# Second-layer weights and tables ahead of the filter loads, eight tiles turned by DMA, a first tile copied by two engines, and a new planned order

## The chip, the core and the metric

The kernel runs on one core of one Trainium2 chip. The metric is device time in microseconds (us), the median over runs of the same program. The core has five engines that run side by side, each working through its own list of instructions strictly in order: PE (TensorE, matmuls), DVE (VectorE), ACT (ScalarE), POOL (GpSimd) and SP (SyncE, which here only issues transfers). Transfers between device memory and the on-chip buffer (SBUF) are carried by 16 DMA engines; SP, ACT and POOL can issue them. Matmuls write to PSUM, a small memory of eight banks, from which ACT or DVE copy the results out ("evacuate" them).

## What is computed

The output is the sum of three things: x itself, a spectral filter of the layer-normalised x (a two-dimensional real FFT, a product with complex weights W, the inverse FFT), and a two-layer perceptron of the same normalised x with a tanh GELU. x has 2048 rows and 640 columns, W 2048 x 321, the hidden layer 1536 columns; everything is bf16.

```python
def _A_ref(x, w_r, w_i):
    X = rfft2(x.astype(float32), axes=(-2, -1))
    X = X * (w_r + 1j * w_i)
    return irfft2(X, s=(S, D), axes=(-2, -1)).astype(bfloat16)

def _B_ref(x, w1, b1, w2, b2):
    h = gelu(einsum("bsd,df->bsf", x, w1) + b1)
    return einsum("bsf,fd->bsd", h, w2) + b2

x = A_x
xn = layernorm(x, axis=-1)
return x + _A_ref(xn, A_w_r, A_w_i) + _B_ref(xn, B_w1, B_b1, B_w2, B_b2)
```

## The kernel before

**Tiles.** x is held as 16 tiles of 128 rows (tile c has the rows 16p + c). The FFTs are matmuls with constant tables: G and H along the rows, E and GE along the columns, and the small M and N that join the sixteen tiles.

**Stage 1, tile by tile (DVE leads).** A tile is loaded (load_x). DVE takes its mean and variance (bn_stats, L567; bn_aggr, L569; ve = variance + 1e-5, L571). POOL raises ve to the power -1/2 (rstd, L572). DVE forms nmr = -mean x rstd (L574) and the normalised tile (L595). PE turns the tile over, five 128 x 128 transposes against an identity (L607), into one PSUM bank, and DVE or ACT copies it into xnT (L486 or L485, called from L612). The same normalised tile is folded on DVE (L618, L622) and multiplied by G on PE (L628), and the result goes into XV (L634). The buffers of normalised tiles hold two pairs of tiles (p_xn), so a pair takes the place of the pair two before it.

**Stage 2, the perceptron's first layer.** Blocks of 1, 1, 2, 2, 2, 4 and 4 tiles (BLOCKS) times 12 pieces of 128 hidden columns: five matmuls into one PSUM bank (L650), then a GELU on ACT into gT (L656). These sums have four banks to rotate through (ZONE "hps"). W1 arrives in three pieces (W1P).

**Stage 3, the spectral chain.** Its PE pieces have a fixed order (CHAIN): b pieces multiply XV by E and need XV of all sixteen tiles, c pieces apply M, DVE multiplies by the filter Wf (L723) and subtracts and adds (L727), d pieces apply N, copies bring the result into U, and SP turns U back into XV with DMA transposes (L748). Wf has 34 loads (load_w), 17 from A_w_r and 17 from A_w_i, and the first product waits for all of them.

**Stage 4, the second layer and the end.** Each output tile is a sum of 12 pieces gT x W2 (the function `second`), of H x the spectral result, of b2 and of x. For eight tiles (KEEP) gT x W2 is done ahead and added to b2bc by DVE (L824); for the other eight ACT copies b2bc (L803) into the place of the output. Either way POOL then adds x by an accumulating DMA (L826). b2bc is b2 spread to all 128 partitions by its load. DVE makes the last sum (L835), and SP stores (L838).

**The order.** The program is not written in the order in which it runs. Every operation is handed to a planner (Sched) with the engines that may do it, an estimated duration, a priority, and what it reads and writes. `schedule` runs through time with these estimates and, engine by engine, picks the operation that can start first, by priority among those within 0.03 us; it also decides, for a copy that DVE or ACT may do, which does it. For SP it keeps the order in which the operations were written down. A `gate` lets an operation be placed only after another one was placed; it is no wait on the chip, and neither is `late`, the earliest planned time. `sync` then puts semaphore waits where the data need them, and `emit` writes the five lists. On the chip an engine that reaches a wait stops, with all that is behind it in its list. All estimates bear on the order alone.

SP's list is thus: x tile 0, identity, tile 1, b1, W1's second piece, tiles 2 and 3, W1's third piece, G, the tiles 4 to 15 in pairs, E, M, N, the 34 filter loads, W2, GE, H, b2bc, then the transposes of U and the stores. ACT's list begins with the first piece of W1 (its DMA), then a table load for copies, and one for GELU ahead of the first GELU. POOL's has all nine rstd first, then the sixteen accumulating DMAs.

Of the kernel before, what the change touches and what calls it, by code (L numbers as in the profile page):

```python
# [13 lines left out]
D = 640  # L14
# [83 lines left out]
def act_us(n, ptr=0):  # L98
    return 0.055 + n / 1200.0 + 0.09 * ptr
# [57 lines left out]
class Sched:  # L157
# [36 lines left out]
    def schedule(self):  # L194
# [24 lines left out]
        while left:  # L219
            best = None  # L220
            for e in self.engines:
# [27 lines left out]
                if e == "sp":  # L249
                    t, o = min(cands, key=lambda c: c[1].seq)  # L250
                    if o is not min((p for p in pend[e] if not p.done), key=lambda p: p.seq):
                        continue
                else:
                    t0 = min(c[0] for c in cands)
                    near = [c for c in cands if c[0] <= t0 + 0.03]
                    if e == "pe" and self.mode != "128":
                        near = [c for c in cands if c[0] <= t0 + HOLD and c[1].alts and c[1].alts[0][0][0] == self.mode] or near
                    t, o = min(near, key=lambda c: (-c[1].prio, c[1].seq))
# [13 lines left out]
            if o.nbytes:  # L272
                if e == "pool":
                    o.end = t + 5.0
                else:
                    s = max(t + 0.9, dma_free)
                    dma_free = s + o.nbytes / o.rate
                    o.end = dma_free + 0.9
            else:
                o.end = t + dur + LAT[e]  # L280
# [96 lines left out]
W1P = [(0, 5), (5, 8), (8, 12)]  # L377
GROUPS = [(0, 2), (2, 3), (5, 3), (8, 3), (11, 3), (14, 2)]
BYDMA = ()
# [3 lines left out]
PRIO = {"hps": 10, "gelu": 50, "pb": 70, "pc": 80, "filt": 85, "ipc": 90, "eps": 60, "fin": 40}  # L383
# [4 lines left out]
HOME = (KEEP[:max(0, len(KEEP) - 7)] + tuple(c for c in range(15) if c not in KEEP))[:8]  # L388
WARM = (55, 12)


def bass_parallel_sum__spectral_gfnet__dense_activation_gelu__prompt_kernel(
# [21 lines left out]
    with ExitStack() as es:  # L414
# [27 lines left out]
        nmr = sb("nmr", [128, 16], F32)  # L442
# [25 lines left out]
        def load(dst, src, buf, nbytes, after=(), reads=(), rate=395e3, q="sp"):  # L468
            return K.op([(q, 0.45)], 400, lambda e, _: e.dma_start(dst, src), reads=reads, writes=[buf], after=after, nbytes=nbytes, rate=rate)  # L469
# [20 lines left out]
        K.op([("dve", 0.1)], 300, lambda e, _: e.memset(warm[:], 0.0), writes=[B_warm])  # L490
        K.op([("pool", 0.1)], 100, lambda e, _: e.memset(mhalf[:], -0.5), writes=[B_mh])
# [16 lines left out]
        def load_x(c, n, q="sp"):  # L508
            o = load(view(X, c * D, [[1, n * D]]), xv[:, c:c + n, :].rearrange("p c d -> p (c d)"), B_x[c], n * D * 256, q=q, rate=155e3 if c == 0 else 395e3)
            for i in range(1, n):  # L510
                B_x[c + i].writers.append(o)

        def load_w1(j, q="sp"):
            a, b = W1P[j]
            load(view(W1, 128 * a, [[F, 5], [1, 128 * (b - a)]]), w1v[:, :, 128 * a:128 * b], B_w1s[j], 163840 * (b - a), q=q, rate=300e3)
# [7 lines left out]
        load_w1(2)  # L523
        load(gtab[:], const["G"], B_g, 524288)
        for c in range(4, 16, 2):
            load_x(c, 2)
        load(etab[:], const["E"], B_e, 204800, rate=250e3)
        load(mtab[:], const["M"], B_m, 65536, rate=70e3)
        load(ntab[:], const["N"], B_n, 49152, rate=70e3)
        WP = 32 * KP  # L530

        def load_w(wsrc, p0, off, row, n, step):
            load(bass.AP(tensor=Wf, offset=p0 * WP + off, ap=[[2 * WP, 16], [2 * KP, n], [1, 321]]),
                 bass.AP(tensor=wsrc.tensor, offset=wsrc.offset + row * 321, ap=[[128 * 321, 16], [step * 321, n], [1, 321]]),
                 B_w, 16 * 642 * n, after=[wpad], rate=165e3)
# [12 lines left out]
        load(W2[:], w2v, B_w2, F * D * 2)  # L548
        load(getab[:], const["GE"], B_ge, 204800)
        load(htab[:].rearrange("p a b -> p (a b)"), const["H"], B_h, 524288)  # L550
        load(b2bc[:], bass.AP(tensor=b2v.tensor, offset=b2v.offset, ap=[[0, 128], [1, D]]), B_b2b, 163840)
# [3 lines left out]
        K.op([("dve", 0.08)], 200, lambda e, _: e.tensor_copy(b1col[:], psb(B_b1ps.slot, [[1, NFC]])), reads=[B_b1ps], writes=[B_b1c])  # L555
# [3 lines left out]
        norm_ops, ring_ops, a_ops = [], [], []  # L559
        B_rs = [Buf(f"rstd{c}") for c in range(16)]  # L560
        for c0, n in [(0, 1), (1, 1)] + [(c, 2) for c in range(2, 16, 2)]:
            pr = 100 - c0 / 2
            B_mv, B_ve, B_r = Buf("mv"), Buf("ve"), Buf("r")
            for c in range(c0, c0 + n):
                B_st = Buf("st")
                for h in range(2):
                    K.op([("dve", 0.393)], pr, lambda e, _, c=c, h=h: e.bn_stats(stats[:, c, 6 * h:6 * h + 6], view(X, c * D + H2 * h, [[1, H2]])),  # L567
                         reads=[B_x[c]], writes=[B_st])
# [4 lines left out]
                 reads=[B_ve, B_mh], writes=[B_r])  # L573
            K.op([("dve", 0.071)], pr, lambda e, _, a=a, b=b: e.scalar_tensor_tensor(out=nmr[:, a:b], in0=mv[:, a:b, 0], scalar=-1.0,  # L574
                                                                                     in1=rstd[:, a:b], op0=ALU.mult, op1=ALU.mult),
                 reads=[B_mv, B_r], writes=B_rs[a:b])
            for c in range(a, b):
                B_rs[c].writers += B_r.writers

        for pair in range(8):  # L580
# [10 lines left out]
            for n in range(2):  # L591
# [4 lines left out]
                    out=xnv(n, 0, [[1, D]]), in0=view(X, c * D, [[1, D]]), scalar1=rstd[:, c:c + 1], scalar2=nmr[:, c:c + 1], op0=ALU.mult, op1=ALU.add),  # L596
                    reads=[B_x[c], B_rs[c]], writes=[xn, B_xn])
                norm_ops.append(o)
                if c in BYDMA:
                    K.op([("sp", 1.6)], 0, lambda e, _, c=c, n=n, xnv=xnv: e.dma_start_transpose(xnT[:, :, 128 * c:128 * c + 128], xnv(n, 0, [[1, D]])),  # L600
                         reads=[B_xn, xn], writes=[B_xnT[c]], nbytes=163840, rate=150e3)
                    continue
                tps = Buf(f"tps{c}", psum, 1, ZONE["tps"])

                def xt(e, _, n=n, xnv=xnv, tps=tps):
                    for j in range(5):
                        ins = e.transpose(psb(tps.slot, [[1, 512]]).bitcast(BF)[:, 128 * j:128 * j + 128], xnv(n, 128 * j, [[1, 128]]), ident[:])  # L607
                    return ins
                tp = K.op([("pe", 5 * mm_us(128))], pr, xt, reads=[B_xn, xn, B_id], writes=[tps], alts=[[("128", 5 * mm_us(128))]])
                if not c:  # L610
                    idle(WARM[1], WARM[1] * mm_us(128), gate=[tp])
                K.op([("dve", 0.41), ("act", act_us(640))], pr,  # L612
                     copy(lambda c=c: xnT[:, :, 128 * c:128 * c + 128],
                          lambda tps=tps: psb(tps.slot, [[1, 512]]).bitcast(BF)[:, 0:640].rearrange("p (j t) -> p j t", j=5)),
                     reads=[tps], writes=[B_xnT[c]])
# [54 lines left out]
        def five_segs(n):  # L670
            return [("128", 4 * n * mm_us(Q4)), ("32", n * 0.075 + 0.01)]
# [5 lines left out]
        for gi, (c0, n) in enumerate(GROUPS):  # L677
# [8 lines left out]
            for v in range(2):  # L686
                K.op([("dve", dve_us(320 * n) + 0.05), ("act", act_us(320 * n) + 0.16)], PRIO["pb"] - c0 / 10,
# [184 lines left out]
```

## Time and profile before

| what | value |
|---|---|
| median of three runs | 157.81 us (157.73 to 157.98) |
| the profiled execution: span | 160.8 us |
| PE busy | 148.7 us (92% of the span) |
| DVE busy | 113.2 us (70%) |
| ACT busy | 84.0 us (52%) |
| POOL busy | 26.2 us (16%) |
| mean granted PE clock | 0.979 |

All views are of one profiled execution. It is 2.99 us longer than the median of the plain runs. In the profile a line such as `L474 PE MATMUL ps<-xnT,W 128*128 128x256 bf16 x40` reads: source line, engine, operation, what is written and read, shape, how many; PEld are the weight loads that go with the matmuls. Line 474 is the helper through which nearly all matmuls go, so they are told apart by their tiles: xnT,W is the first layer, W,gT the second, gtab,T the product with G, etab,XV the b pieces, Xb,mtab the c pieces, Z,ntab the d pieces, getab,XV and Wf,htab the way back. A "landing" is the time from the issue of a transfer to its completion.

Transfers of the first 40 us, from the view of DMA issues (KB, and us from issue to landing):

| transfer | queue | issued at | KB | to landing |
|---|---|---|---|---|
| x tile 0 | SP | 0.74 | 160 | 2.9 |
| W1, first piece | ACT | 0.74 | 800 | 5.2 |
| identity | SP | 1.21 | 32 | 4.9 |
| x tile 1 | SP | 1.66 | 160 | 4.8 |
| W1, second piece | SP | 2.61 | 480 | 5.7 |
| x tiles 14 and 15 | SP | 7.62 | 320 | 13.5 |
| E | SP | 8.10 | 200 | 14.6 |
| A_w_r, 17 loads | SP | 9.76 to 23.9 | 80 each | 9.3 (median) |
| A_w_i, 17 loads | SP | 24.57 to 35.8 | 80 each | 2.6 (median) |
| W2 | SP | 36.43 | 1920 | 9.7 |
| H | SP | 38.01 | 512 | 9.9 |
| b2bc | SP | 38.53 | 160 | 9.8 |

### The profile page before, as it was taken

The numbers are of one execution on the slowest core, as the hardware profiler recorded it, in microseconds if no ns is written. First come the engines' busy times: TensorE is split into PE (matmuls) and PEld (weight loads), VectorE is DVE, ScalarE is ACT, GpSimd is POOL, SyncE is SP. The second block draws the span as 40 slices with busy tenths as digits, with TensorE's granted clock in tenths as the row PEclk, the third lists the DMA queues.
The fourth block names the chain that finished last, engine by engine and source line by source line (L and its number), as shares of the span: only waits on it lengthen the run. The fifth ranks groups of instructions, "written<-read, shape, count | busy, mean of one in ns | idle before, by whom it ended". The sixth has DMA issues, their size and how long they took to land.

```text
span 160.8 us, 4316 instructions
## 1 busy us (share of the span) xinstructions
PE 148.7 (92%) x1823; PEld 98.4 (61%) x1845; DVE 113.2 (70%) x258; ACT 84.0 (52%) x147; POOL 26.2 (16%) x33
## 2 busy tenths in 40 slices
PE   7979999999981999998999999998999999999994
PEld 7969899999850356464465355443447664665563
DVE  1659999999993024589995786991206999998222
ACT  3288989899709655353246884356865451211000
POOL 1112101111027600302113045202006000000000
PEclk9999999999997589999999999999999999999999
DMA  5999995458941940051649509996651914222112
GB/s 143 356 380 394 212 140 121 105 128 202 378 189 20 207 99 4 4 84 34 131 81 161 90 4 156 208 166 126 138 115 18 167 64 161 86 86 82 41 56 66
DMA packets 30394, 21.71 MB, mean 135 GB/s; under 512 B 12712, under 2 KB 28200, under 8 KB 30376
## 3 DMA queue, kind: packets, MB, share of 16 engines
q1 hardware_dynamic: 23320, 15.39, 38.4%
q0 software_dynamic: 6400, 5.24, 20.2%
q10 hardware_dynamic: 656, 0.82, 1.4%
q8 instruction: 14, 0.23, 0.6%
q14 instruction: 4, 0.03, 0.1%
HBM read 13.58 MB, written 2.62 MB: 101 GB/s over the span
## 4 chain that ended last, share of the span: by engine, by line
PE 57%; SPq 22%; DMA 8%; DVE 4%; ACT 4%; issue 3%; DVEq 0%
PE ps L474 57%; SPq L469 22%; DMA b2bc<-in_B_b_dram 6%; DVE T L723 2%; DMA XV<-U 2%; ACT gT L656 2%; ACT Wf L485 1%; DVE Z L727 1%; ACT xnT L803 1%; DVE Y L486 1%; DVEq L359 0%; ACT U L485 0%; DVE X L824 0%; DVE W L835 0%; SPq L748 0%
## 5 line engine op out<-in xcount | busy, mean ns | idle before, releaser
L474 PE MATMUL ps<-xnT,W 128*128 128x256 bf16 (+2 forms) x413 | 57.8, 294 | 6.0 <-ACT gT L656 4.6
L474 PE MATMUL ps<-W,gT 128*128 128x128 bf16 (+3 forms) x382 | 55.2, 292 | 1.6 <-issue 1.3
L474 PEld LDWEIGHTS ps<-xnT,W 128*128 128x128 bf16 x420 | 35.8, 99 | 23.2 <-ACT gT L656 6.3
L656 ACT ACTIVATE gT<-ps,b1col 128x256 bf16<-128x256 f32 (+2 forms) x84 | 39.7, 506 | 8.8 <-PE ps L474 6.8
L474 PEld LDWEIGHTS ps<-W,gT 128*128 128x128 bf16 x396 | 29.8, 98 | 23.3 <-issue 2.4
L826 POOL DMA_DIRECT2D xnT<-in_A_x_dram x8 | 12.3, 1785 | 33.0 <-ACT xnT L803 23.5
L567 DVE BATCH_NORM_STATS2 stats<-X 128x6 f32<-128x320 bf16 x32 | 14.3, 472 | 2.9 <-DMA X<-in_A_x_dram 2.9
L485 ACT ACTIVATE Wf<-ps 128x960 bf16<-128x960 f32 (+1 forms) x9 | 7.6, 878 | 15.5 <-PE ps L474 15.5
L723 DVE TENSOR_TENSOR T<-Y,Wf 128x1288 bf16<-128x1288 bf16 x16 | 12.4, 821 | 0.8 <-issue 0.8
L572 POOL TENSOR_TENSOR rstd<-ve,mhalf 128x2 f32<-128x2 f32 (+1 forms) x9 | 6.3, 699 | 38.1 <-DVE ve L571 38.1
L485 ACT ACTIVATE Xb<-ps 128x960 bf16<-128x960 f32 (+1 forms) x7 | 7.9, 1157 | 8.0 <-PE ps L474 7.8
L826 POOL DMA_DIRECT2D X<-in_A_x_dram x8 | 7.0, 873 | 27.1 <-DVE X L824 25.6
L485 ACT ACTIVATE XV<-ps 128x1280 bf16<-128x1280 f32 (+1 forms) x8 | 9.3, 1157 | 2.9 <-PE ps L474 2.7
L835 DVE TENSOR_TENSOR W<-ps,xnT 128x640 bf16<-128x640 f32 x8 | 6.5, 819 | 5.6 <-PE ps L474 5.4
L485 ACT ACTIVATE Y<-ps 128x644 bf16<-128x644 f32 x8 | 5.7, 707 | 8.5 <-PE ps L474 8.5
L486 DVE CAST Wf<-ps 128x960 bf16<-128x960 f32 (+1 forms) x3 | 3.1, 1044 | 8.6 <-PE ps L474 8.6
L486 DVE CAST Y<-ps 128x644 bf16<-128x644 f32 x8 | 6.6, 825 | 3.6 <-PE ps L474 3.6
L622 DVE TENSOR_TENSOR T<-T 128x512 bf16<-128x512 bf16 (+1 forms) x32 | 8.5, 315 | 0.0
L486 DVE CAST Xb<-ps 128x960 bf16<-128x960 f32 (+1 forms) x5 | 5.5, 1098 | 4.1 <-PE ps L474 4.1
L485 ACT ACTIVATE U<-ps 128x512 bf16<-128x512 f32 (+1 forms) x12 | 4.6, 435 | 7.1 <-PE ps L474 4.6
L835 DVE TENSOR_TENSOR W<-ps,X 128x640 bf16<-128x640 f32 (+2 forms) x10 | 6.7, 683 | 1.9 <-PE ps L474 1.9
L474 PE MATMUL ps<-getab,XV 32*128 32x160 bf16 (+1 forms) x128 | 7.6, 242 | 0.0
(47 smaller groups left out, 147.7 us busy)
## 6 DMA issues: line engine op xcount, KB each, us to landing
xnT<-in_A_x_dram POOLq DMA_DIRECT2D x8, 320.0 KB, 4.9
X<-in_A_x_dram POOLq DMA_DIRECT2D x8, 320.0 KB, 5.1
out_dram<-W SPq DMA_DIRECT2D x15, 160.0 KB, 1.8
X<-in_A_x_dram SPq DMA_DIRECT2D x7, 320.0 KB, 10.2
W<-in_B_w_dram SPq DMA_DIRECT2D x1, 1920.0 KB, 9.7
Wf<-in_A_w_r_dram SPq DMA_DIRECT2D x15, 80.2 KB, 9.3
Wf<-in_A_w_i_dram SPq DMA_DIRECT2D x15, 80.2 KB, 2.6
W<-in_B_w_dram ACTq DMA_DIRECT2D x1, 800.0 KB, 5.2
```

The lines of the kernel that those rows point to most:

```text
L469: return K.op([(q, 0.45)], 400, lambda e, _: e.dma_start(dst, src), reads=reads, writes=[buf], after=after, nbytes=nbytes, rate=rate)
L474: ins = e.matmul(o_, lhsT=lw, rhs=rh, start=st, stop=sp_, skip_group_check=True)
L485: return e.activation(dst(), src(), ACT.Copy, scale=scale)
L486: return e.tensor_copy(dst(), src())
L567: K.op([("dve", 0.393)], pr, lambda e, _, c=c, h=h: e.bn_stats(stats[:, c, 6 * h:6 * h + 6], view(X, c * D + H2 * h, [[1, H2]])), reads=[B ...
L572: K.op([("pool", 0.65)], pr, lambda e, _, a=a, b=b: e.tensor_tensor(out=rstd[:, a:b], in0=ve[:, a:b], in1=mhalf[:, a:b], op=ALU.pow), read ...
L622: ring_ops.append(K.op([("dve", dve_us(4 * w, 2))], pr, lambda e, _, op=op, x1v=x1v, xfv=xfv, o_=o_, o0=o0, o1=o1, w=w: e.tensor_tensor(ou ...
L656: K.op([("act", act_us(128 * nt, 1))], pr + PRIO["gelu"], lambda e, _, c0=c0, nt=nt, fc=fc, hps=hps: e.activation(gT[:, fc, 128 * c0:128 * ...
L723: filt_ops.append(K.op([("dve", dve_us(4 * KP, 2))], pr, lambda e, _, k=k, Y=Y, TB=TB, pair=pair: e.tensor_tensor(out=view(TT, TB.slot * 8 ...
L727: K.op([("dve", dve_us(2 * KP, 2))], pr, lambda e, _, TB=TB, Z=Z, r=r, op=op: e.tensor_tensor(out=view(Zb, Z.slot * 4 * KP + r * KP, [[2 * ...
L826: K.op([("pool", 1.5)], 51, lambda e, _, c=c, xov=xov, shaped=shaped: e.dma_start(xov(0, D), shaped(xv[:, c, :]), accum_op=ALU.add), reads ...
L835: K.op([("dve", dve_us(w))], 95, lambda e, _, os_=os_, fps=fps, o0=o0, w=w, xov=xov, shaped=shaped, base=base: e.tensor_tensor(out=shaped( ...
```

## The change

Loads: W1's pieces are 3, 4 and 5 hidden columns instead of 5, 3 and 4. x tiles 4 and 5 come ahead of G. W2 (now in two halves), b2bc, GE and H are planned ahead of the filter loads; the planner gives the filter loads the earliest time 19 us (WLATE). SP's operations now have priorities like those of the other engines: transposes 500, stores 450, loads 400.

Tiles 8 to 15 (BYDMA) are not turned by PE and copied: SP turns them from the normalised tile straight into xnT, by DMA. Tile 0 is turned in two parts, three blocks that DVE copies and two that ACT copies. nmr is gone: the normalised tile is (x - mean) x rstd in one DVE instruction. The GELU table is loaded as ACT's first instruction, ahead of the DMA of W1's first piece, and b1's copy is ACT's. Several planned durations change, the priority of the first layer goes from 10 to 45, and a gate that kept the first kept tile of the second layer behind the first b piece is dropped.

```diff
-W1P = [(0, 5), (5, 8), (8, 12)]
+W1P = [(0, 3), (3, 7), (7, 12)]
-BYDMA = ()
+BYDMA = tuple(range(8, 16))
-PRIO = {"hps": 10, "gelu": 50, ...
+PRIO = {"hps": 45, "gelu": 50, ...
+WLATE = 19.0
...
-                if e == "sp":
-                    t, o = min(cands, key=lambda c: c[1].seq)
-                    if o is not min((p for p in pend[e] if not p.done), key=lambda p: p.seq):
-                        continue
-                else:
-                    t0 = min(c[0] for c in cands)
...
+                t0 = min(c[0] for c in cands)
...
+        K.op([("act", 1.3)], 410, lambda e, _: e.preload_act_table(ACT.Gelu_apprx_tanh), writes=[Buf("table")])
...
         load_w1(2)
+        load_x(4, 2)
         load(gtab[:], const["G"], B_g, 524288)
-        for c in range(4, 16, 2):
+        for c in range(6, 16, 2):
             load_x(c, 2)
+        for h in range(2):
+            load(W2[:, 6 * h:6 * h + 6, :], w2v[:, 6 * h:6 * h + 6, :], B_w2, F * D)
...
+        load(b2bc[:], bass.AP(tensor=b2v.tensor, offset=b2v.offset, ap=[[0, 128], [1, D]]), B_b2b, 163840)
...
-                 B_w, 16 * 642 * n, after=[wpad], rate=165e3)
+                 B_w, 16 * 642 * n, after=[wpad], rate=165e3, issue=0.645, late=WLATE))
...
-        load(W2[:], w2v, B_w2, F * D * 2)
         load(getab[:], const["GE"], B_ge, 204800)
         load(htab[:].rearrange("p a b -> p (a b)"), const["H"], B_h, 524288)
-        load(b2bc[:], bass.AP(tensor=b2v.tensor, offset=b2v.offset, ap=[[0, 128], [1, D]]), B_b2b, 163840)
...
-        K.op([("dve", 0.08)], 200, lambda e, _: e.tensor_copy(b1col[:], psb(B_b1ps.slot, [[1, NFC]])), reads=[B_b1ps], writes=[B_b1c])
+        K.op([("act", 0.2)], 200, lambda e, _: e.activation(b1col[:], psb(B_b1ps.slot, [[1, NFC]]), ACT.Copy), reads=[B_b1ps], writes=[B_b1c])
...
-            K.op([("dve", 0.071)], pr, lambda e, _, a=a, b=b: e.scalar_tensor_tensor(out=nmr[:, a:b], ...
...
-                    out=xnv(n, 0, [[1, D]]), in0=view(X, c * D, [[1, D]]), scalar1=rstd[:, c:c + 1], scalar2=nmr[:, c:c + 1], op0=ALU.mult, op1=ALU.add),
+                    out=xnv(n, 0, [[1, D]]), in0=view(X, c * D, [[1, D]]), scalar1=mv[:, c, 0:1], scalar2=rstd[:, c:c + 1], op0=ALU.subtract, op1=ALU.mult),
...
+                if not c:
+                    st_ops[2].gate.append(o)
                 if c in BYDMA:
-                    K.op([("sp", 1.6)], 0, lambda e, _, c=c, n=n, xnv=xnv: e.dma_start_transpose(xnT[:, :, 128 * c:128 * c + 128], xnv(n, 0, [[1, D]])),
-                         reads=[B_xn, xn], writes=[B_xnT[c]], nbytes=163840, rate=150e3)
+                    ring_ops.append(K.op([("sp", 1.3)], 500, lambda e, _, c=c, n=n, xnv=xnv: e.dma_start_transpose(xnT[:, :, 128 * c:128 * c + 128], xnv(n, 0, [[1, D]])),
+                         reads=[B_xn, xn], writes=[B_xnT[c]], nbytes=163840, rate=200e3))
...
+                for j0, j1, engs in ((0, 3, ["dve"]), (3, 5, ["act"])) if c == 0 else ((0, 5, ["dve", "act"]),):
+                    nj = j1 - j0
+                    tps = Buf(f"tps{c}", psum, 1, ZONE["tps"])
...
-                    second(c, kps, 0, D, pr, ([kept_ops[-2]] if len(kept_ops) > 1 else [pb_ops[0]]) + [l1_of[j][-1] ...
+                    second(c, kps, 0, D, pr, ([kept_ops[-2]] if len(kept_ops) > 1 else []) + [l1_of[j][-1] ...
```

What the planner makes of it, as the built lists have it:

- SP: the loads up to tiles 14 and 15, both halves of W2, E, M, b2bc, N, GE, H, the 17 loads from A_w_r, the transposes of tiles 8 and 9, three loads from A_w_i, tiles 10 and 11, two loads, tiles 12 and 13, three loads, tiles 14 and 15, the last nine loads, then the transposes of U and the stores. Each transpose waits for its normalised tile.
- ACT: the first copy of b2bc (L805) stands after 24 GELUs of 128 columns and 12 of 256, before another 24 of 256; three more follow before the first b piece's copies. No second table load.
- POOL: the first accumulating DMA stands between the rstd of tiles 6 and 7 and that of 8 and 9, the second between those of 11 and 12, the others follow the last rstd.
- DVE: one bn_stats of tile 1 stands between bn_aggr and ve of tile 0. The normalisation of tile 12 waits for the transposes of tiles 8 and 9, that of tile 14 for those of 10 and 11.
- PE: 24 second-layer matmuls stand ahead of the first b piece (none before), and 15 first-layer matmuls of 512 columns instead of 35; after it the remaining first-layer pieces are spread over the whole chain, the last of them behind the first two pieces of the way back.

## The prediction

> **What bounds the kernel now.** The page first: PE (the matmuls) is busy 92% of a 160.8 us span, so only PE's idle time, its clock and its work can shorten the end. Its slices of 4.02 us show where it is not at full work:
>
> ```profile
> ## 2 busy tenths in 40 slices
> PE   7979999999981999998999999998999999999994
> ACT  3288989899709655353246884356865451211000
> PEclk9999999999997589999999999999999999999999
> ```
>
> Slice 13 (48 to 52 us) has PE at 1, slices 13 to 15 have the granted clock at 0.7, 0.5 and 0.8; the start (slices 1 to 3) is thin too. The view of waits for 44 to 58 us names the cause, and the timeline gives times:
>
> ```profile
> ACT xnT L803 <- DMA b2bc<-in_B_b_dram: 4.4, 1, 4.4
> PE ps L474 <- ACT gT L656: 3.9, 1, 3.9
> ...
> 48.34 0.74 ACT L803 ACTIVATE xnT<-b2bc 128x640 f32<-128x640 bf16 x1 [4.44 <-DMA b2bc<-in_B_b_dram]
> 51.49 5.73 PE L474 MATMUL ps<-xnT,W 128*128 128x512 bf16 x13 [3.91 <-ACT gT L656]
> 57.85 1.46 PE L474 MATMUL ps<-xnT,W 128*128 128x512 bf16 x6
> 112.50 7.73 PE L474 MATMUL ps<-xnT,W 128*128 128x512 bf16 x34
> ```
>
> ACT runs in order. Its copy of b2bc (L803) waits from 43.9 to 48.34 for the last load of the SP queue; the gelus (L656) stand behind it, and PE, with no PSUM bank for more first-layer sums, stops from 47.58 to 51.49. Then 13 matmuls of 512 columns take 5.73 us, 441 ns each, where 34 others take 227 each: the windows of 1 us show the clock at 0.50 from 51 to 57. Elsewhere PE idles little.
>
> **The change, part by part, against the span of 160.8 us.** The page gives this execution's span alone; it is 2.99 us above the median of the runs (157.81), and I carry this distance over.
>
> *1. The stall.* b2bc, W2, getab and htab now stand ahead of the 34 filter loads in the SP queue. Gone: 3.91 us of idle, 0.42 us just before it (PE busy 0.58 of the microsecond 47 to 48), and the half clock, 13 x (0.441 - 0.227) = 2.8. Together 7.1.
>
> [...]
>
> *2. Eight tiles (8 to 15) turned by DMA.* PE loses 8 x 5 = 40 matmuls of L607. Ten of them hold PE's weight loads 0.60 us, 60 ns each, in a stage where PE is busy in every window from 18 to 42 us: 40 x 0.06 = 2.4 us. DVE loses eight copies (0.44 us net, two take 0.87) and nine nmr of 0.16. I count nothing for them: DVE is as full as PE there, but it is PE's work that makes the end. The lines are of the timeline (all engines, then SP's queue), the last of the view of SP's transposes:
>
> ```profile
> 26.00 0.60 PEld L607 LDWEIGHTS ps<-ident,T 128*128 128x128 bf16 x10
> 26.06 0.72 PE L607 MATMUL ps<-ident,T 128*128 128x128 bf16 x10
> 26.63 0.87 DVE L486 COPY xnT<-ps 128x640 bf16<-128x640 bf16 x2
> ...
> 81.05 2.63 SPq L748 DMA_TRANSPOSE XV<-U  x2
> 98.41 5.17 SPq L748 DMA_TRANSPOSE XV<-T  x2
> DMA to landing us min/median/max: 2.6/3.3/7.4
> ```
>
> The price moves to SP: each transpose holds the queue 1.2 to 2.6 us (two in 2.63, two in 5.17) and lands 2.6 to 7.4 us after issue.
>
> [...] In this trace the DMA moved 176 GB/s from 84 to 88 us, with four transposes and two POOL transfers in flight; I go by the rows.
>
> *3. The start.* The gelu table is loaded first, not at 7.92 us ahead of the first gelu: PE's idle 0.70 at 8.93 goes. The first tile's copy, 0.70 us on ACT, is split over two engines, and nmr leaves the chain to the first tile (0.16 plus its handover). Against it, one bn_stats of tile 1 now stands before ve of tile 0 on DVE and waits for the second x load (landed 1.66 + 4.8 = 6.46 before; W1's first piece is now 480 KB instead of 800 and later, so x should land sooner). The bounds: lost 0.8 if that load lands as before (6.46 + 0.43 against ve at 4.81 is 2.1 late, less 0.2 for nmr, 0.35 for the split, 0.70 for the table), won 1.7 (0.70, 0.35, 0.2 and the 0.47 that PE idles at 11.2 for the second tile). I take 0.9 won, by the table load's row.
>
> *4. New waits.* Three places, each with its queue:
> - ACT: the first copy of b2bc stands after 24 small and 12 middle gelus, which ended at 26.17 before, so at about 25.3. Ahead of b2bc are 7.4 MB. By the full rate (5.12 MB moved by 16 us, then 0.39 MB/us) it lands at 22.2; by the late tail of the last x load (5.14 MB landed at 21.1) at 29.8; by the rate of W2 to b2bc (2.86 MB from 38.9 to 48.3, 304 GB/s) at 27.2. Wait 0 to 4.5; I take 1.3, less than the last, since PE has four banks of slack. Behind it: the gelus, so PE; and on POOL the accumulating DMA (L828) with rstd of tiles 8 and 9 behind it, so DVE.
> - SP: transposes of tiles 8/9, 10/11, 12/13, 14/15 each wait for DVE's normalised tile (30.2 to 46.0 before, some 0.5 to 3 earlier now) and hold back the 17 A_w_i loads between and after them. PE wants tiles 8 to 11 at 43.1 - 30 x 0.06 - 0.9 = 40.4. Tile 11 is issued at about 37 (ready near 34.5; ahead of it three loads of 0.6 and two transposes); with the median landing 3.3 that is 40.3, with the extremes 38.7 to 47. Wait 0 to 6; I take 0.6. DVE's normalisation of tiles 12 and 14 reuses the slots of 8 and 10 and waits for the same landings, at about 38.5 and 42.5: covered.
> - DVE: the first product with the filters (L725). Its stage starts at 59.14 - 7.1 - 2.4 - 0.9 - 4.5 + 3.6 = 47.8 (20 matmuls of 512 less and 24 second-layer ones more ahead of it), and PE works 8 us and a copy 0.8 until the product is due at 57. The last nine loads go out behind tile 15 (43.5 + 2.6), 0.65 us each: issued by 52, landed by 55. Covered by 2; the cover also has to hold four POOL transfers of 2.0 us of all DMA engines each (74.5% of 11 us for four from 49 to 60).
>
> Everything behind 57 us keeps its work; its pieces change places in a stage where PE already idles only 0.2 to 0.5 us at a time: between 1.5 won and 1.5 lost, taken as nothing.
>
> **Sum:** 160.8 - 7.1 - 2.4 - 0.9 + 1.3 + 0.6 = 152.3 us of span; minus 2.99, **149.3 us**.
>
> **The rivals.**
> *A, the transposes on PE were hidden anyway.* ACT now does, before that stage, 24 small gelus (0.29), 36 middle (0.49), 3 large (0.69), seven XV copies (six of 1.24, one of 0.6), four b2bc copies (0.74) and three others: 39 us of work in the 39.4 us from 8.4 to 47.8. In 18 to 42 us it was 90% busy. If it can't exceed that, it takes 43.3 us and the stage starts at 51.7, with 1.0 for b2bc at 52.7: 4.9 lost where the sum has 1.9. For it: it is full; against: its idle time before was a wait for PE. Time 152.3.
> *B, late tiles.* Tiles 8 to 11 land by the bad row (7.4, so at 44.4), PE idles 4 us and takes the half clock's 2.8 as well: 149.3 + 4 - 0.6 + 2.8 = 155.5.
> *C, slower than before: the filters land too late.* If each of eight transposes holds SP 2.6 us as at 98.41, with the POOL transfers in flight, the queue needs 10.4 us more and the last filter lands at 65 or later; DVE and PE wait from 57. An idle of 7.6 us plus 2.8 of clock gives back all 10.4: from a landing at about 64.6 on the change loses. At 66: 149.3 - 1.9 + 9 + 2.8 = 159.2. Against: in 24 to 38 us the DMA engines were only about half busy, and two transposes together took 2.5 to 3.4 us in seven of eight cases.
> *D, no new wait and the small idles close too:* 149.3 - 1.9 - 1.5 = 145.9.
> That the change does not do what it says is excluded for the order: the built order has b2bc as the 19th load of SP, ahead of all 34 filter loads, where it was the 55th and last.
>
> **How the numbers follow.** Forecast (147 to 151.3) 0.52, A 0.16, B 0.13, C 0.10, D 0.09. The prediction is the forecast's 149.3. The range runs from D (145.8) to 153.5, which leaves out C and most of B, 0.2; the forecast's own is 147 to 151.3. Within 0.2% (0.3 us, what a measurement here can tell from none) lies only a sliver between B and C: 0.02. Faster 0.88, slower 0.10.
>
> **What would show it.** Right: no PE gap over 1 us between 44 and 60, PEclk at 9 throughout, 40 fewer L607 matmuls, the first product with the filters at 57 to 59 and waiting for PE, not for DMA. Part 3: first xnT matmul by 7.7 us and no idle before the tenth. Part 4: ACT's wait for b2bc and PE's wait for xnT by DMA, each under 1.5. Wrong: a DVE wait for the filter loads, a half-clock window, or SP transposes of 2.6 us each.

## The result, and the profile after

| | before | after |
|---|---|---|
| median | 157.81 us (20 runs) | 157.62 us (20 runs) |
| ratio after to before | | 0.994 [0.991, 0.997] |
| the profiled execution: span | 160.8 us | 156.1 us |
| mean granted PE clock in it | 0.979 | 1.000 |
| first b piece (PE) in it | 59.14 us | 49.90 us |
| from the first b piece to the end of the span | 101.7 us | 106.2 us |

The ratios leave out runs more than 1.5% above the fastest of the same kernel (8 of the changed kernel's 20 here, three of twelve in experiment 1, ten of twelve in 5, three of six in 8, two of six in 12); the medians leave out none.

The change wins about half a per cent by the ratio and 0.2 us by the medians, where 149.3 us was predicted. Yet against the profile of before the first b piece starts 9.24 us earlier, at 49.90, and the prediction's steps (47.8, and 1.9 of new waits) give 49.7. That it is so close is partly luck: the new waits are 0 and 1.76 us where 1.3 and 0.6 were taken. Two things went wrong: the span fell by 4.7 us only, and the median did not follow even that.

The page of the changed kernel, slices of 3.9 us:

```profile
## 2 busy tenths in 40 slices
PE   7999999999599999799999999969999999999993
ACT  3078989899773745536466365535569300230000
PEclk9999999999999999999999999999999999999999
```

The stall and the half clock are gone. What is thin now are three other places: slice 11 (42 us), slice 17 (66 us) and slice 27 (104 us). PE's waits from 40 to 130 us (us in total, times, longest):

```profile
PE ps L469 <- ACT xnT L805: 1.8, 1, 1.8
PE ps L469 <- ACT U L480: 1.5, 1, 1.5
PE ps L469 <- DVE Xb L481: 0.7, 2, 0.5
PE ps L469 <- DVE X L826: 0.6, 2, 0.5
PE ps L469 <- DVE W L837: 0.5, 1, 0.5
PE ps L469 <- ACT gT L658: 0.3, 1, 0.3
```

And the timeline at the places that the prediction named (start, duration; in brackets the idle time before and what ended it):

```profile
25.02 0.73 ACT L805 ACTIVATE xnT<-b2bc 128x640 f32<-128x640 bf16 x1
42.28 2.97 PE L469 MATMUL ps<-xnT,W 128*128 128x512 bf16 x13 [1.76 <-ACT xnT L805]
49.90 0.96 PE L469 MATMUL ps<-etab,XV 128*128 128x160 bf16 x16
59.83 2.31 DVE L725 TENSOR_TENSOR T<-Y,Wf 128x1288 bf16<-128x1288 bf16 x3 [1.04 <-DMA Wf<-in_A_w_i_dram]
103.76 0.52 PE L469 MATMUL ps<-Z,ntab 32*32 32x320 bf16 x32 [1.48 <-ACT U L480]
```

ACT's copy of b2bc has no wait: b2bc landed at 24.5. The 13 matmuls take 2.97 us and not 5.73. PE waits 1.76 us ahead of them. The view names ACT's copy, but the transposes say otherwise: tile 11, turned by DMA, was issued at 36.70 and landed at 42.20, and these matmuls read it. The 1.04 us ahead of DVE's product is no wait for a filter either, though the view says so (experiment 5). At 103.76 the last d piece waits for U to be copied, which waits 2.2 us for DMA transposes to leave its buffer. Behind the first b piece PE's waits sum to 3.6 us; before they were 1.1 (0.36, 0.49 and 0.28; eleven gaps of 0.16 us with no cause but "issue" are left out, since that profile lists 18 matmuls fewer there than weight loads). The way from the first b piece to the end is 4.5 us longer: 2.5 are these waits, 0.9 is work that the prediction moved there itself (its 4.5 less 3.6), and the rest no view here settles.

### The profile page after: what moved, and what is told of

Its sections match the earlier page's. It is cut to its first block, busy times and chain, and to the rows that moved or that the text cites. A ratio compares the mean times of both kernels' runs of the same rounds, so it can differ in the third digit from the quotient of the medians.

```text
span 156.1 us, 4256 instructions
## 1 busy us (share of the span) xinstructions
PE 146.9 (94%) x1805; PEld 95.2 (61%) x1805; DVE 112.7 (72%) x243; ACT 79.4 (51%) x145; POOL 26.5 (17%) x33
## 4 chain that ended last, share of the span: by engine, by line
PE 69%; DVE 11%; DMA 7%; ACT 4%; SPq 4%; issue 2%; DVEq 1%; POOL 0%
PE ps L469 68%; DMA XV<-U 5%; DVE T L725 4%; SPq L750 3%; DMA X<-in_A_x_dram 2%; DVE Z L729 2%; ACT XV L480 2%; PE ps L608 1%; DVE Xb L481 1%; DVE T L481 1%; ACT U L480 1%; DVE X L826 1%; DVE W L837 1%; DVEq L354 1%; DVE Y L481 1%
## 5 line engine op out<-in xcount | busy, mean ns | idle before, releaser
L469 PE MATMUL ps<-xnT,W 128*128 128x256 bf16 (+2 forms) x420 | 57.0, 288 | 2.4 <-ACT xnT L805 1.8
L469 PE MATMUL ps<-W,gT 128*128 128x512 bf16 (+3 forms) x396 | 58.1, 295 | 1.0 <-DVE W L837 0.5
L469 PEld LDWEIGHTS ps<-xnT,W 128*128 128x128 bf16 x420 | 34.4, 98 | 18.1 <-ACT gT L658 2.1
L480 ACT ACTIVATE Wf<-ps 128x960 bf16<-128x960 f32 (+1 forms) x8 | 6.7, 868 | 18.3 <-PE ps L469 18.3
L480 ACT ACTIVATE Xb<-ps 128x960 bf16<-128x960 f32 (+1 forms) x6 | 6.8, 1134 | 8.2 <-PE ps L469 8.2
L481 DVE CAST Wf<-ps 128x960 bf16<-128x960 f32 (+1 forms) x4 | 4.3, 1072 | 8.6 <-PE ps L469 8.6
L480 ACT ACTIVATE U<-ps 128x512 bf16<-128x512 f32 (+1 forms) x14 | 5.4, 434 | 9.1 <-PE ps L469 6.9
L480 ACT ACTIVATE XV<-ps 128x1280 bf16<-128x1280 f32 (+1 forms) x7 | 8.0, 1145 | 2.5 <-PE ps L469 2.4
L481 DVE CAST Xb<-ps 128x960 bf16<-128x960 f32 (+1 forms) x6 | 6.8, 1125 | 2.4 <-PE ps L469 2.4
L591 DVE TENSOR_SCALAR T<-X,mv,rstd 128x640 bf16<-128x640 bf16 x16 | 7.1, 456 | 1.6 <-POOL rstd L573 1.4
```

What stands on the lines that cost most here:

```text
L469: ins = e.matmul(o_, lhsT=lw, rhs=rh, start=st, stop=sp_, skip_group_check=True)
L480: return e.activation(dst(), src(), ACT.Copy, scale=scale)
L481: return e.tensor_copy(dst(), src())
L591: o = K.op([("dve", 0.356)], pr, lambda e, _, c=c, n=n, xnv=xnv: e.tensor_scalar(out=xnv(n, 0, [[1, D]]), in0=view(X, c * D, [[1, D]]), sc ...
```

## The experiments

All ratios are to the kernel before, with their 95% intervals. A kernel's timed runs each have a span too, and the time is about 1.8 us above it in all of them (1.73 to 1.86; these spans are given to 0.1).

**1. The kernel before, once more.** No edit.

> The kernel before, unchanged, with a new profile and with the span and clock of every counted run. Theory 1 (the profiled execution of before was not like the counted ones): the runs of the changed kernel stand 1.77 us above their spans (157.86 against 156.1); if that holds here too, the median of 157.81 means a span of 156.0, not 160.8, the mean clock of most counted runs is 1.000 and not 0.979, and the half clock (2.8 us) and part of the 3.91 us stall are missing from a new profile, where the first b piece starts at 54 to 57 and not at 59.14. Rival (offset): stall and half clock are in the ordinary runs as well, the clock is 0.98 in most of them, the new profile has its first b piece at 59 again, and the 2.99 us are something else between a span and a run.

Measured: 157.83 us; 0.998 [0.995, 1.001]. Of 35 executions of it in this comparison 28 had a clock of 0.999 or 1.000, with a median span of 156.0 us; seven had 0.989. The new profile fell on one of those seven, span 158.9. Its timeline, and its windows (busy shares of PE, PEld, DVE, ACT and POOL, then PEclk, DMA share, GB/s):

```profile
46.79 0.74 ACT L803 ACTIVATE xnT<-b2bc 128x640 f32<-128x640 bf16 x1 [2.83 <-DMA b2bc<-in_B_b_dram]
49.94 4.67 PE L474 MATMUL ps<-xnT,W 128*128 128x512 bf16 x13 [2.31 <-ACT gT L656]
56.51 0.97 PE L474 MATMUL ps<-etab,XV 128*128 128x160 bf16 x16
```
```profile
50.00:51.00 1.00, 1.00 (x4) 0.34 (x5) 0.00 (x0) 1.00 (x2) 1.00 (x2) 0.61 0.85 124
51.00:52.00 1.00, 1.00 (x4) 0.41 (x3) 0.00 (x0) 0.63 (x1) 1.00 (x2) 0.50 1.45 214
52.00:53.00 1.00, 1.00 (x4) 0.30 (x2) 0.00 (x0) 0.95 (x2) 0.58 (x1) 0.50 1.36 203
53.00:54.00 1.00, 1.00 (x4) 0.40 (x3) 0.00 (x0) 0.37 (x2) 0.34 (x1) 0.68 1.41 207
```

So theory 1 holds: most runs have no half clock, and the stall is not one number. It was 3.91 us in the execution profiled first and 2.31 in this one, both with the half clock. How long it is in a run at full clock no profile shows. An execution with a span of 160.8 us takes 162.6; none of the 20 runs timed against the change was that slow (the slowest 160.93; one later run took 162.44).

**2. The loads alone.** The kernel before; after planning, SP's list is rearranged and nothing else:

```diff
+        early = [o for o in sp if o.name in ("w2", "i", "h", "b2")]
+        rest = [o for o in sp if o not in early]
+        at = min(k for k, o in enumerate(rest) if o.name == "W")
+        K.order["sp"] = rest[:at] + early + rest[at:]
```

> The kernel before with one thing changed: in the SP queue the loads of W2, getab, htab and b2bc stand ahead of the 34 filter loads; the order of PE, DVE, ACT and POOL is the same instruction by instruction. If the stall at 47.6 to 51.5 (3.9 us, and 0.4 ahead of it) is in the ordinary runs and its end is carried to the end of the kernel, this alone gives 157.8 - 4.3 = 153.5 (ratio 0.973), and with the half clock in the ordinary runs 150.7 (0.955). If what the stall costs is given back behind it (the filters land some 10 us later and PE waits there, or the chain has a floor of its own), 157.0 to 158.5 (0.995 to 1.005), and the profile shows the wait: DVE for Wf or ACT and PE behind it.

Measured: 155.67 us (155.09 to 155.71); 0.986 [0.982, 0.991]. Neither case: 2.1 us are won. PE works through at 47.28 and reaches the first b piece at 52.17:

```profile
47.28 2.98 PE L474 MATMUL ps<-xnT,W 128*128 128x512 bf16 x13
52.17 0.97 PE L474 MATMUL ps<-etab,XV 128*128 128x160 bf16 x16
```

Against the first profile of before that is 6.97 us earlier, and the span of 153.8 is 7.0 us shorter: of that execution the prediction's 7.1 was nearly right, and nothing was given back behind it. Against an ordinary run (a clock of 0.999 or 1.000, median span 156.0) it is 2.2. One part of the change, alone, does better than the whole.

**3. All tiles turned on PE.** The changed kernel, planned anew:

```diff
-BYDMA = tuple(range(8, 16))
+BYDMA = ()
```

> The changed kernel with all sixteen tiles turned on PE (none by DMA); the list scheduler orders everything anew. If the tiles turned by DMA are what costs (SP's queue is full from 0.7 to 54.7 us, PE waits 1.76 at 42.3 and DVE 1.04 for the last filter at 59.8), the waits of 2.8 us go and 40 x 0.06 = 2.4 us of PE work come back: 157.2, between 156 and 158 (ratio to before 0.99 to 1.00). If the DMA turns won their 2.4 us cleanly: 160.0 (1.014).

Measured: 159.72 us; 1.010 [1.004, 1.017]. Against this the change, with eight tiles turned by DMA, wins 2.1 us (2.6 by the ratios), so the turns are no loss as such. What they win is not shown: four of these six runs had a clock of 0.988 or 0.989, the other two took 158.36 and 157.82, near the change, and the lists differ as well. The profile's largest wait, 2.67 us, is for a U tile at the way back, with the half clock behind it.

**4. The old priority.** The changed kernel, planned anew:

```diff
-PRIO = {"hps": 45, ...
+PRIO = {"hps": 10, ...
-... if len(kept_ops) > 1 else []) + [l1_of...
+... if len(kept_ops) > 1 else [pb_ops[0]]) + [l1_of...
```

> The changed kernel with the old priority of the first layer (hps 10, not 45) and the old gate of the first second-layer sums on the first b piece, so that the chain of b, c and d pieces is laid among the other work as before. If the new order is what loses the time behind the first b piece (PE idles 3.6 us there, 1.1 before, and the way from the first b piece to the last matmul is 103.8 us against 99.3): 157.6 - 2.5 = 155 (ratio to before 0.982), first b piece near 50 and last matmul within 100 to 101.5 us of it. If the order is not it: 157.6 +- 0.7 with the waits of the end in other places.

Measured: 158.98 us; 1.005 [1.001, 1.009]. A miss: with the other planned durations the planner does not return to the old order. This third order is worse by eight of its twelve runs, which had a clock of 0.989; the four at 1.000 took 157.15 to 158.08, like the change. In its profile a d piece waits for DVE's Z, while DVE works without a gap from 93.4 us on, and the half clock begins at 100.49:

```profile
100.45 0.76 PE L469 MATMUL ps<-Z,ntab 32*32 32x320 bf16 x32 [1.88 <-DVE Z L729]
```

The U tiles issued at 88.7 to 91.5 landed 6.8 to 7.9 us later; that this wait comes of them is not shown.

**5. Filters on a second queue.** The changed kernel with the last eight filter loads issued by POOL. The expectation says that PE, DVE and ACT keep their order; in the traces they do not quite: the planner moved a few operations of each (PE's weight loads differ in four places).

```diff
+            on_pool = len(WL) >= 26
...
+ ... q="pool" if on_pool else "sp"))
+            if on_pool:
+                WL[-1].prio = 60
```

> The changed kernel with the last eight filter loads issued by POOL (between its other work, from about 20 us on) and not by SP; PE, DVE and ACT keep their order instruction by instruction. In the profile of the changed kernel SP issued the last nine at 48.4 to 54.7, the last landed at 59.65 and DVE's first filter product waited 1.04 for it; PE idled 0.28, 0.53 and 0.47 behind that (62 to 66.4). If the late filters cost that time, the product waits for PE and no DMA and the time falls by 1.0 to 1.3: 156.4 (ratio to before 0.986 where the change has 0.994). If the chain behind has the same floor anyway: 157.6 (0.994).

Measured: 160.02 us (155.92 to 165.44); 0.992 [0.985, 0.998]. A miss that taught two things. The filters landed by 52.9, and yet the product stood behind an idle time of 1.04 us again and PE behind its 0.28, 0.53 and 0.47. So PE's three waits are not for the filters (experiment 6 has them too, with the change's own lists on PE, DVE, ACT and SP). Nor is the 1.04: in the chain of the changed kernel DVE's queue steps there through 19 semaphore waits (L354 is `wait_ge`), 0.1 us each and without a pause, from 57.97 to 59.78. The last filter landed at 59.65. The end of that row:

```profile
59.73 0.05 DVEq L354
59.78 0.04 issue
59.83 2.31 DVE T L725 x3
```

The kernel before has 0.84 there, with 17 such waits, and experiment 9, in the old order, has the same 1.04:

```profile
59.13 2.31 DVE L743 TENSOR_TENSOR T<-Y,Wf 128x1288 bf16<-128x1288 bf16 x3 [1.04 <-issue]
```

The second thing: with the loads among POOL's work the turned tiles landed up to 8.9 us after issue, so that DVE's normalisation of tile 12 waited, PE behind it, and seven of twelve runs fell to a clock of 0.98 or 0.99:

```profile
40.59 0.45 DVE L594 TENSOR_SCALAR T<-X,mv,rstd 128x640 bf16<-128x640 bf16 x1 [2.15 <-DMA xnT<-T]
41.23 0.73 PE L469 MATMUL ps<-gtab,T 128*128 128x128 bf16 x10 [1.82 <-DVE T L627]
```

**6. POOL's transfers held.** The changed kernel; PE, DVE, ACT and SP keep their lists:

```diff
-                     reads=[xb2], writes=[xo], nbytes=327680, rate=150e3)
+                     reads=[xb2], writes=[xo], nbytes=327680, rate=150e3, after=[zone["c01"]])
```

> The changed kernel with the accumulating transfers of POOL (L828, 320 KB each) held until the second c piece (57.35 us in its profile); PE, DVE, ACT and SP keep their order instruction by instruction. In the changed kernel five of them went out at 26.05, 35.93, 42.64, 46.26 and 51.22, among the tiles turned by DMA and the filter loads; in the kernel before, with only its loads moved, three went out at 45.3 to 50.1 and one at 50.3. If they are what holds the turned tiles and the filters back (tile 11 landed 5.5 us after its issue at 36.7 and PE waited 1.76 for it; the last filter landed 5.5 after its issue at 54.1), tile 11 lands by 40.5, the last filter by 57.5, both waits fall under 0.3 and the time falls by 2.5 to 3: 154.8 (ratio to before 0.978). If it is SP's own queue and the turning itself, the waits stay and the time is 157.6 (0.994); if the transfers only collide later, with the U tiles, 158 to 159.

Measured: 155.74 us; 0.989 [0.983, 0.994]. Where the changed kernel had these on POOL,

```profile
26.05 1.66 POOL L828 DMA_DIRECT2D xnT<-in_A_x_dram  x1 [2.77 <-ACT xnT L805]
35.93 1.53 POOL L828 DMA_DIRECT2D xnT<-in_A_x_dram  x1 [2.13 <-ACT xnT L805]
42.64 1.52 POOL L828 DMA_DIRECT2D xnT<-in_A_x_dram  x1
46.26 0.89 POOL L828 DMA_DIRECT2D X<-in_A_x_dram  x1 [2.10 <-ACT X L805]
51.22 1.50 POOL L828 DMA_DIRECT2D xnT<-in_A_x_dram  x1 [4.07 <-DVE xnT L826]
```

there is none before 56.31 now. The landing of the eight turned tiles, first in the changed kernel, then here:

```profile
DMA to landing us min/median/max: 2.7/4.3/5.5
```
```profile
DMA to landing us min/median/max: 2.7/2.9/4.4
```

Tile 11, issued at the same time (36.75), landed after 2.65 us, PE's wait of 1.76 is gone, and the first b piece starts at 47.98. The filters landed by 56.1, and the idle times of 0.28, 0.54 and 0.47 stayed, as in experiment 5. U still waited, 1.11.

**7. Four tiles turned by DMA.** The changed kernel with `BYDMA = tuple(range(12, 16))`, planned anew.

> The changed kernel with four tiles turned by DMA (12 to 15) and 8 to 11 on PE; all is ordered anew. PE gets back 20 x 0.06 = 1.2 us of work and loses the wait of 1.76 for tile 11, and SP has 5.2 us less to issue ahead of the last filters, so that the wait of 1.04 goes too. If those waits are the loss: 157.6 + 1.2 - 1.8 - 1.0 = 156.0 (0.984). If the turns by DMA are a plain gain of 2.6 us for eight, as the comparison of sixteen tiles on PE (159.7) with the change shows: 157.6 + 1.3 = 158.9 (1.002).

Measured: 156.78 us, all twelve runs within 156.71 and 156.93; 0.994 [0.991, 0.997]. Between the two cases and not apart from the change. In its profile PE waits for no turned tile, and the spread of the changed kernel (155.5 to 160.3) is gone as well; why is not shown.

**8. The old order, all parts.** The changed kernel with the lists of PE, DVE, ACT and POOL taken from the kernel before, but for the first stage; SP is planned as in the change:

```diff
+FORCED = {"pe": [...], "act": [...], "dve": [...], "pool": [...]}
...
+                    if e in FORCED and key[o] != FORCED[e][place[e]]:
+                        continue
```

> The changed kernel with the order of PE, DVE, ACT and POOL of the kernel before, given as lists (only the first 16 to 35 us, to the third and fourth tile pair, keep the new order; the transposes of tiles 8 to 15 and their copies are left out of the lists, since DMA turns them). If the new order is what loses 3.6 us behind the first b piece, this has the gains of all parts: 155.7 (the loads alone) - 2.4 (turned tiles) - 0.5 (start) + 0.3 = 153.1 (ratio to before 0.970), first b piece at 49 to 50.5, and 101.5 to 102 us from it to the end as with the loads alone. If the loss comes with the tiles turned by DMA themselves (SP's queue, late filters), 156 to 158 with waits for Wf, xnT or U in the same places.

Measured: 155.06 us (152.98 to 157.17); 0.974 [0.967, 0.980]: by the ratios two per cent faster than the change, with the same loads, turned tiles and start. The profile is of a run at 156.47, and shows what is left. PE, POOL's transfers, and the landing of U's transposes:

```profile
104.21 0.52 PE L487 MATMUL ps<-Z,ntab 32*32 32x320 bf16 x32 [2.47 <-ACT U L498]
```
```profile
84.88 3.04 POOL L846 DMA_DIRECT2D xnT<-in_A_x_dram  x2 [8.07 <-ACT xnT L823]
88.12 0.90 POOL L846 DMA_DIRECT2D X<-in_A_x_dram  x1 [0.20 <-issue]
92.06 0.86 POOL L846 DMA_DIRECT2D X<-in_A_x_dram  x1 [3.04 <-DVE X L844]
```
```profile
DMA to landing us min/median/max: 2.4/4.3/11.1
```

The two U transposes issued at 88.2 and 89.6 landed 11 us later, while four of POOL's transfers were under way.

**9. The old order, transfers held.** Experiment 8 with POOL's transfers of tiles 8 to 12 behind the last turned U tile, the others behind the second c piece; every engine keeps its list:

```diff
-... rate=150e3)
+... rate=150e3, after=[u_turn if c in (8, 9, 10, 11, 12) else zone["c01"]])
```

> The old order with all parts of the change (155.06 before), and the accumulating transfers of POOL held: those of tiles 8 to 12 until the last turned U tile has landed, the rest until the second c piece. PE, DVE, ACT, SP and POOL keep their order. If the transfers are what makes U tiles land late (those issued at 85.5 to 89.6 landed 6.6 to 11.2 us later while four transfers went out at 84.9 to 92.1, and PE waited 2.47 us for U at 104.2, at half clock behind it), U tiles land within 5 us, the wait falls under 0.5 and the time to 152.5 (ratio to before 0.966), with a narrower spread than 152.98 to 157.17. If the turns delay one another, the wait stays and the time is 155 (0.982); if the held transfers come too late for the final sums, 155 to 157 with DVE L837 waiting for them behind 120 us.

Measured: 153.30 us (152.5 to 153.8); 0.970 [0.966, 0.975], the fastest kernel here. U's transposes land within 4.1 us, and PE's d piece follows without a wait:

```profile
DMA to landing us min/median/max: 2.4/2.6/4.1
```
```profile
101.50 0.51 PE L487 MATMUL ps<-Z,ntab 32*32 32x320 bf16 x32
```

**10. The new order, transfers held.** The same edit in the changed kernel; only POOL's list differs from the change.

> The changed kernel (its own order on PE, DVE, ACT and SP) with the same holds on POOL's transfers. With the first hold alone it took 155.7, and PE waited 1.11 for U at 101.5. If the transfers cause that wait too: 154.7 (ratio to before 0.981), U wait under 0.3, and what is left against the old order are the PE idles of 1.3 at 60 to 65, 0.33 at 88 and 0.53 at 123 (2.1 us): 2 us above the old order with the same holds. If the U wait is of the new order itself: 155.7.

Measured: 154.36 us (154.18 to 155.81); 0.981 [0.976, 0.987]. The time is as expected, the reason only in part. The profile (of a run at 155.81) still has U's wait, with no transfer of POOL's near:

```profile
PE ps L469 <- ACT U L480: 1.5, 1, 1.5
PE ps L469 <- DVE X L826: 0.9, 2, 0.5
PE ps L469 <- DVE Xb L481: 0.7, 2, 0.5
```

U has three buffers, and the copy waits for a transpose to leave one: it was issued at 96.50 and took 4.57 us, and the last transfer of POOL's had been issued at 89.30 and landed at 93.20. Four of the six runs were some 1.5 us faster than this one; whether they lack the wait, no profile shows.

**11. The loads, transfers held.** Experiment 2 with the same holds.

> The kernel before with the loads moved (155.67) and the same holds: no tile turned by DMA, the old start, the old order. It lacks only the turned tiles, the start and the planner's prices against the old order with all parts and the holds. If the transfers cost it the 0.42 at 105 us alone: 155.2 (0.983). The difference to the old order with all parts and holds is then what turned tiles and start are worth without collisions: by the prediction's steps 2.4 + 0.9 = 3.3, by the rows (2.4, and the start 0.5) 2.7.

Measured: 155.96 us (155.46 to 156.26); 0.988 [0.985, 0.992]. Without turned tiles in the way the holds bring nothing. It differs from experiment 9 by the turned tiles, the start and the planner's order of the first stage and of SP's loads: 2.66 us.

**12. Two transfers let go earlier.** Experiment 9 with tiles 9 and 12 behind an earlier U tile:

```diff
+... B_ut[15] if c in (8, 10, 11) else B_ut[11] if c in (9, 12) else zone["c01"]
```

> The old order with all parts and the holds (153.3), but the transfers of tiles 9 and 12 wait for the U tile of the third pair group (landed 91.9) and not for the last one (109.9). In the kernel with all five held, seven transfers went out at 110.2 to 114.5, the last landed 11.8 us after its issue, DVE's final sum (L855) stood idle 1.91 us ahead of 126.74 and PE waited 0.49 and 0.79 behind it. If the queue of held transfers is what is late there, five go out at 110 and the last lands by 122; PE wins up to 1.2 us: 152.3 (ratio to before 0.965). If the two transfers let go at 92 hold the U tiles of 96 to 100 (landing 2.4 to 4.0 there), PE waits at 101 for U and the time is 153.3 to 154.5 (0.970 to 0.978).

Measured: 155.77 us (154.82 to 158.46); 0.982 [0.975, 0.989]. I had the landing wrong: that U tile landed at 104.0, not at 91.9. So both transfers went out just ahead of the last three transposes, and this is the plainest look at the collision. The three runs at full clock took 154.8 to 154.9, so it costs some 1.5 us even there. Page, POOL and PE (of a run at 158.46):

```profile
PEclk9999999999999999999999999999857999999999
```
```profile
104.30 3.04 POOL L847 DMA_DIRECT2D xnT<-in_A_x_dram  x2 [27.53 <-DMA XV<-gtab]
114.24 1.71 PE L487 MATMUL ps<-getab,XV 128*128 128x160 bf16 x16 [3.63 <-DMA XV<-U]
```

The transposes issued at 104.83, 106.28 and 107.73 landed 6.8, 7.2 and 6.5 us later; in experiment 9, issued within 0.3 us of the same times, they took 2.8, 2.6 and 2.4. PE waits 3.63 us ahead of the way back, and the clock is halved from 112.74 on.

## Why the prediction was wrong

The medians lead from before to after in five steps, each between two kernels that differ in the thing named (the numbers are those of the experiments):

| step | kernels | us, by medians | us, by ratios |
|---|---|---|---|
| loads ahead of the filters | before, 2 | 157.81 to 155.67: -2.14 | -2.2 |
| (transfers held, no turned tiles) | 2, 11 | +0.29 | +0.3 |
| turned tiles, start, order of the first stage | 11, 9 | -2.66 | -2.8 |
| new order | 9, 10 | +1.06 | +1.7 |
| transfers no longer held | 10, after | +3.26 | +2.0 |

The ratios are taken times 157.81. The sum of the last two, some 4 us, is firmer than their parts.

- **Part 1, "Together 7.1", and "minus 2.99": the largest error, 5.0 us.** This is the step that failed. Both numbers come from one execution with the longer stall and the half clock. The span's distance to the median was not an offset: it was the half clock and the longer part of the stall, less the 1.8 us that every run has above its span. Taking off the stall and then the distance counts the same time twice. In an ordinary run the loads are worth 2.14 us (experiment 2). The half clock's 2.8 us were two lengths of 3.41 us, in part over the stall itself; one costs 1.7 (3.41 at half speed; the 13 matmuls of experiment 1 lose 1.69), and most runs have none. There is a slip inside the 7.1 too: the idle of 3.91 us begins at 47.58, so the 0.42 of that microsecond is already in it, and 6.7 remain.
- **Parts 2 and 3, 2.4 and 0.9: right in size.** The first first-layer matmul comes at 8.07, not by 7.7 as named (7.65 before); the idle times of 0.70 and 0.47 behind it are gone. The first 256-column matmul, behind the same 218 matmuls, moves from 17.83 to 16.77 in the change: 1.06 us for the start. PE's first 512-column matmul, with 30 transposes less ahead of it, comes at 40.51 in experiment 9 and at 43.73 in experiment 11; of that 3.22, 1.56 was there already at the 256-column one, so 1.66 for 30, or 0.055 each. Together the two kernels differ by 2.66 where the sum has 3.3.
- **Part 4.** ACT's wait for b2bc (1.3) did not come: b2bc landed at 24.5, between the estimates of 22.2 and 27.2, and the copy stood at 25.02. PE's wait for tiles 8 to 11 (0.6) did, with 1.76 us, well inside its bounds; PE wanted them at 40.5 and tile 11 went out at 36.7, as forecast, but it took 5.49 us and not 3.3. The filters (rival C) were not late for anything: experiments 5 and 6 land them 6.8 and 3.6 us earlier and the same idle times stay. A reading that nothing rests on: from 84 to 88 us three transposes were in flight, not four (the first landed at 83.74).
- **What part 4 named and did not price.** It listed POOL's accumulating transfers as queued behind b2bc. With b2bc landing at 24.5 and not at 48.3 ACT's first copy of it could go to 25.02, and they start at 26.05 and not at 49.38, in the midst of the turned tiles. The early load allows this, the new order does it: with the loads alone they start at 45.27 (experiment 2), in the old order with all parts at 42.79 (8). Experiment 6 holds them back and removes PE's wait without touching any other engine's list.
- **"Everything behind 57 us keeps its work … taken as nothing": the second error.** The new order costs PE waits at 62 to 66, 90, 104 and 125 us. Experiments 9 and 10 put 1.1 us on the order (1.7 by the ratios). Which of its changes does it stays open: the old priority did not bring the old order back (experiment 4).
- **The rivals.** A (ACT full) did not occur: the first b piece came in time. B is the closest in place, half in size, and by a cause that it did not name. D's smooth chain comes nearest in experiment 9, where PE still waits four times behind the first b piece (0.3 to 0.8 us), though at 153.3 and not at 145.9, mostly because of the first error.

## What to carry to other kernels

Before a gain is taken off a profiled span, ask whether that execution is like the timed ones: a span several us above the median minus the usual distance held a disturbance here (160.8 us where 156.0 was usual), and what is removed may be part of it. A load that comes earlier can also start what waits for it (with the loads alone POOL's transfers begin at 45.27 us and not at 49.38); look where those transfers fall, here above all beside DMA transposes (6.5 to 7.2 us to landing in experiment 12, 2.4 to 2.8 in 9). And a planner's new order is a change of its own: force the old order to see what the other parts are worth.

## What the runs showed of the hardware

- DMA transposes of 160 KB landed late among the accumulating transfers of POOL. With the same lists on PE, DVE, ACT and SP, and issued within 0.3 us of the same times, three took 2.4 to 2.8 us without and 6.5 to 7.2 us with two such transfers in flight (experiments 9 and 12). Over the 224 transposes of U in all fourteen profiles: 2.4 to 4.6 us (median 2.6) where none overlapped, 2.4 to 7.2 (4.0) where two did, 2.5 to 11.2 (6.9) where three to five did. The counts alone prove no cause, since a late landing overlaps more; the pair does.
- The half clock came in two lengths here, 3.41 and 6.83 us. Summed over the windows, (1 - PEclk) x 2 is 3.4 us in experiment 1 (0.39 + 0.50 + 0.50 + 0.32 = 1.71) after a wait of 2.31 us, and the 13 matmuls lose 1.69 us. The trace's clock records give 3.41 us there and in experiments 3 (wait 2.67), 4 (1.88) and 8 (2.47), and 6.83 us in the first profile of before (3.91) and in experiment 12 (3.63). After waits of 1.76 and 1.82 us (after, experiment 5's profile) the clock stayed full.
- Where a wait falls may matter beside its length. By the clock records of these six profiles the change to half comes 13, 13, 28, 29, 31 and 33 times 3.413 us after the first change to full (in the first profile of before 44.37 us after it, and its half clock lasts 6.827 us, twice 3.413). In the stretch of 3.41 us that ends there PE was idle 1.9 to 2.7 us; the waits of 1.76 and 1.82 have at most 1.65 in one stretch counted so. In the four profiles with 3.41 us of half clock PE was already at work again when it began; in the two with 6.83 it resumed 1.2 and 1.5 us later. Those two are also the longest waits, so length and place are not told apart.
- Between runs of the same kernel most of the spread goes with this: of 80 executions of the kernel before beside these experiments, 15 had a clock of 0.989 and took 159.29 to 162.44 us; the others took 156.31 to 158.96, but for one of 379.34 at full clock that nothing here explains.
